# A fused attention and expert kernel: ScalarE's part of the weight conversions, moved within the step

## The chip, the cores and the metric

The kernel runs on one core of a Trainium2 chip. The metric is device time in microseconds (us); of the kernel before there are three runs and one profiled execution. The engines of the core are TensorE (PE), VectorE (DVE), ScalarE (ACT) and GpSimd (POOL); SyncE (SP) issues the transfers. Each engine takes its instructions in the order in which the program issued them.

## What is computed

Attention with two mixings of the heads, followed by an expert layer. In the reference, cut to what matters:

```python
scores = scale * np.matmul(q, k.transpose(0, 1, 3, 2))      # (8, 12, 448, 448)
scores = np.einsum('bhij,hg->bgij', scores, w_pre)
attn = np.exp(scores - np.max(scores, axis=-1, keepdims=True))
attn = attn / (np.sum(attn, axis=-1, keepdims=True) + 1e-09)
attn = np.einsum('bhij,hg->bgij', attn, w_post)
x = np.matmul(attn, v)                                      # to (3584, 768)
y = ((x @ w1) * (x @ w2) @ w3) @ w_out                      # 768 -> 1024 -> 1024 -> 768
```

The four expert weights are 64-bit floats, which the kernel reads as pairs of 32-bit integers and converts on the chip.

## The kernel before, in words

**The steps.** A batch has 448 query rows; a step handles 10 of them for all 12 heads, so a tile has 120 rows, a batch 45 steps and the kernel 360. `run` (L901 on) issues step after step, and within a step the calls stand in a fixed order; that order and the engines' queues set everything. Step n contains, with the names that the profile uses:

- VectorE's `largest(n)`: the minimum `mn` over the mixed scores `psm` (L246; the mixed scores stand there with the sign reversed, so it is the maximum that the softmax subtracts).
- ScalarE's `exp(n)`: `e` and its row sums `sm` (L253). In steps below WHOLE = 20 it is issued right behind `largest`; from step 20 on it is the last call of the step.
- `scale(n-1)`: VectorE's `sa`, `ri` (L262, L263) from the row sums, and `w` (L266), the post-mixing weights times 1/sum.
- `split_r(n+2)`: the scores of a later step in two parts, `rh` (VectorE, L226) and `rl` (GpSimd, L227).
- `qk`: scores of a later batch on TensorE (`psq`, L193, L194), copied by ScalarE to `st` (L198) and stored to DRAM (`raw_d`, L202), from where `fetch` (L217) reads them in the step's layout. In the first steps `qk_first` does the same for batch 0, with ScalarE's copies `sz` (L162, L163).
- `post(n-2)`: TensorE's `pso` (L276, eight matmuls a row block), copied by ScalarE to `mt` (L282) when `do_ends` runs near the step's end.
- `mix(n+1)`: TensorE's next `psm` (L235 in the first 20 steps, L238 to L240 after).
- in some steps `av`: the value products `psa` (L307) from `mt`, in PSUM bank 5. These steps contain no piece of a conversion.
- a share of the expert products (fold products `psf`, L365; expert products `eg`, L527, their copy `ea`, L533, and so on).

**The conversions.** `converting` (L124) is a generator that two passes of a step drive. A job is one block of a weight: `words` loads it (`cs`, L96, SyncE, three buffers) two pieces ahead; `square` (L102, ScalarE) makes `cm` from the top words, which tells where a value would be too small; `to_f32` shifts the words together on VectorE (`ca`, L112 to L114, in PSUM bank 5) and ends with `cx` (L116), which needs `cm`; `two_parts` casts `cx` to a high part on ScalarE (L121) and subtracts it on GpSimd for the low part (L122). There are 72 jobs: 40 for folding w3 with w_out (steps up to 43), then 32 unit jobs for w1 and w2 (steps 48 to 100), whose result is stored by L430 for later batches. In a piece the load of job n+2 comes in the first half of the step, and in the second half, behind the step's `exp` (below step 20), `scale`, `split_r` and `qk`:

```python
            if made:
                jobs[n - 1][1](made)        # cast and low part of job n-1
                made = None
            if 0 <= n < len(jobs):
                s = words.pop(0)
                m = self.square(s, f"{self.n_made}")
                made = self.to_f32(s, m, f"{self.n_made}")
```

The tile of the square has one buffer, the tile of `cx` those of its pool.

Of the kernel before, what the change touches and what calls it, by code (L numbers as in the profile page):

```python
# [6 lines left out]
F32 = mybir.dt.float32  # L7
# [18 lines left out]
WHOLE = 20  # L26
FIRST = 48
CW = 384
# [17 lines left out]
class Kernel:  # L46
# [51 lines left out]

    def square(self, s, name):
        n = s.shape[1]  # L100
        m = self.cx.tile([128, CW], F32, tag="m", name=f"cm{name}", bufs=1)[:, :n]
        self.nc.scalar.activation(m, s[:, :, 1].bitcast(F32), AF.Square)  # L102
        return m

# [16 lines left out]
        self.nc.scalar.copy(hi, x)  # L121
        self.nc.gpsimd.tensor_tensor(lo, x, hi.bitcast(F32), op=ALU.subtract)  # L122

    def converting(self, jobs):  # L124

        words, made = [], None
        jobs = list(jobs)
        for n in range(-2, len(jobs) + 1):  # L130
            if n + 2 < len(jobs):
                src = jobs[n + 2][0]
                words.append(self.words(src, f"{self.n_words}"))
                self.n_words += 1
            yield
            if made:
                jobs[n - 1][1](made)
                made = None
            if 0 <= n < len(jobs):
                s = words.pop(0)  # L140
                m = self.square(s, f"{self.n_made}")
                made = self.to_f32(s, m, f"{self.n_made}")
                self.n_made += 1
            yield

# [598 lines left out]
    def run(self):  # L746
        nc, tc = self.nc, self.tc
        self.kqs, self.parts, self.rs, self.rhl, self.psm, self.mns, self.es, self.w2s = ({} for _ in range(8))
        self.mt, self.vs, self.xs, self.fw = {}, {}, {}, {}
        self.later, self.ends, self.soon = [], [], []  # L750
        self.slot, self.free, self.keep, self.x_made, self.n_groups = {}, list(range(N_UP)), [], [0] * B, 0
        self.jobs, self.ys, self.pairs = [], {}, False
        dp = self.pool("dram", 1, space=DRAM)
# [62 lines left out]
        for b in range(1, B):  # L816
            first, per, ahead = (12, 26 / 48, 2) if b == 1 else ((b - 1) * NB - 6, 45 / 48, 3)
            for u in range(H * NJ):
                h, c = divmod(u, NJ)
                n = first + int(u * per)  # L820
# [36 lines left out]
        for pair in range(ONE // 2, B // 2 - 1):  # L857
            first = P_AT if pair == ONE // 2 else 2 * NB * (pair + 1) + 13
# [5 lines left out]
        def advance(count):  # L864
            nonlocal done
            for _ in range(min(count, total - done)):
                next(background)
                done += 1

        def there(p):  # L870

            f, r = divmod(p - 3 - 2 * KF, 3)
            return 2 * KF * 3 * (1 + f) + (0, 9, 18)[r] if f >= 0 else min(max(3 * (p - 3), 0), KF * 3)
# [3 lines left out]
        def others(p):  # L877
            nc.sync.dma_start(self.kq0s[p][:, JT + S:], self.kq0[p][:, JT + S:])
# [17 lines left out]
        self.unit_list = self.units()  # L896
        self.n_one, self.w_made = len(self.unit_list), 4 * KF
        self.unit_list += self.pair_units()
        unit_pieces, phases = self.converting(self.unit_jobs()), list(self.phases())
        nq, n_pieces = 0, -2  # L900
        for n in range(N + 6):  # L901
            self.step = n
            if n == GB + 1:
                self.close("qp")
                self.xp = [self.pool("xp0", 1)]
            if n == SWITCH:
                assert done == total
                next(background, None)
                self.do_ends()
                self.do_soon()  # L910
                self.do_later()
                assert not fold_pieces
                self.close("fp")
                self.wp = self.pool("wp", 5, side="right")
                self.up = self.pool("up", 1, side="right")
                self.xp.append(self.pool("xp1", 1, side="right"))
                background, total, done = self.experts(phases), (E_1 + E_2) * ONE + P_1 * (B - ONE) // 2, 0
            if n == LATE:
                assert done >= E_1
                self.close("xp0", "cx")  # L920
                self.xq, self.cb = self.pool("xq", 2), self.pool("cb", 1)
            if n == PAIR:

                assert done >= 2 * E_1 + E_2 and unit_pieces is None and not self.jobs and not self.ys
                self.do_ends()
                self.do_soon()
                self.do_later()
                self.pairs, self.w_ahead = True, 4
                self.close("xp1", "cb", "xq", "cs")
                self.xq = self.pool("xq", 2)  # L930
                self.up2 = self.pool("up2", 1, side="right")
                self.free += range(N_UP, NS)
                setup = self.pair_setup(phases)
            if PAIR <= n < PAIR + 7:
                next(setup, None)
            if LF <= n + LF < N:
                self.fetch(n + LF)
            self.do_later()
            if n + 3 < HP:
                others(n + 3)  # L940
            elif 2 * HP - 3 <= n < 2 * HP:
                self.load_v()
            for x in loads.get(n, []):
                self.load_kq(*x)

            p, pieces = self.n_made - 1 if fold_pieces else 2 * KF + 3 * KF, None
            if avs.get(n):
                pass
            elif fold_pieces:
                f = (self.n_made - 1 - 2 * KF) // 3  # L950
                if f < 2 or done >= 2 * KF * 3 * (f - 1):
                    pieces = fold_pieces
                    if next(pieces, self) is self:
                        fold_pieces = pieces = None
            for x in splits.get(n, []):
                self.split_kq(*x, nc.gpsimd, nc.gpsimd)
            if n < N:
                self.largest(n)
            if n < WHOLE:
                self.exp(n)  # L960


            if 0 <= n - 1 < N:
                self.scale(n - 1)
            if n + 2 < N:
                self.split_r(n + 2)
            self.do_soon()
            for x in firsts.get(n, [])[:1]:
                self.later.append(self.qk_first(*x, (next(turn), next(turn))))
            for x in qks.get(n, []):  # L970
                store = self.qk(*x, nq % 2, nc.scalar.copy)
                nq += 1
                if store:
                    self.later.append(store)
            if pieces:
                next(pieces)
            elif unit_pieces and not fold_pieces and not avs.get(n):
                ahead = 1 if n < SWITCH else 2 * done // (3 * K1) + 4 + (done > 0)
                if n_pieces < ahead:
                    n_pieces += 1  # L980
                    if next(unit_pieces, self) is self:
                        unit_pieces = None
                    else:
                        next(unit_pieces)
            now = share.get(n, 0)
            if n < SWITCH:

                wanted += now
                now = max(min(there(p), KF * 3 + wanted) - done, 0)
            self.do_sums()  # L990

            advance(now // 2)
            if 0 <= n - 2 < N:
                self.post(n - 2)
            for x in firsts.get(n, [])[1:]:
                self.later.append(self.qk_first(*x, (next(turn), next(turn))))
            for x in avs.get(n, []):
                self.av(*x)
            advance(now - now // 2)
            if n + 1 < N:  # L1000
                self.mix(n + 1)
            self.do_ends()

            if WHOLE <= n < N:
                self.exp(n)

        self.do_soon()
        self.do_later()
# [61 lines left out]
```

## Time and profile before

| what | value |
|---|---|
| median of 3 runs | 1633.44 us (1632.39 to 1634.12) |
| profiled execution | 1632.78 us, span 1631.0 us |
| TensorE busy | 1577.8 us, 97% of the span |
| VectorE busy | 1028.6 us, 63% |
| ScalarE busy | 1054.1 us, 65% |
| GpSimd busy | 1070.3 us, 66% |
| DMA | 436.47 MB, mean 268 GB/s |

How to read it: the shares are means over stages with different limits. The chain that ended last, followed back from the last instruction, covers only the end of the span, so the stages before it are read from a table of windows: for each stretch of the span the busy time of each engine, the granted clock of TensorE and the share of the DMA engines. In a timeline each row is an instruction with its start, its duration and, in brackets, the idle time of the engine just before it and what ended that idle time.

### The profile page before, as it was taken

To read this page: it belongs to the slowest core of one execution; us is meant where nothing else is said; L and a number is where in the kernel's file an instruction comes from. 1 tells how busy PE (TensorE), PEld (TensorE's weight loads), DVE (VectorE), ACT (ScalarE), POOL (GpSimd) and SP (SyncE) were. 2 spreads that over 40 slices of the span, in tenths; PEclk is the share of its full clock that TensorE was granted. 3 is DMA by queue.
4 is the path that set the end of the run, shared out by engine and by line. 5 is a ranking of instruction groups with operands and counts; after the bars stand their busy time and mean duration, and the time that the engine had idled before them with its cause. 6 is when DMAs were issued, how large, how long until landed. Compare 5 with 4: busy or idle time off the path is not lost. (4 is left out here: it accounts for less than half of the span.)

```text
span 1631.0 us, 31804 instructions
## 1 busy us (share of the span) xinstructions
PE 1577.8 (97%) x10528; PEld 1414.0 (87%) x10528; DVE 1028.6 (63%) x2302; ACT 1054.1 (65%) x2497; POOL 1070.3 (66%) x904
## 2 busy tenths in 40 slices
PE   6989998999999999999999999999999999999999
PEld 2569997888898888889999899998999898999988
DVE  5858668778857777763465465755565557634573
ACT  3878767777867777777776676776775554542321
POOL 1347556667757788885577777876675666655774
PEclk7999999999999999999999999999999999999999
DMA  8989869998899999999988888889988766678875
GB/s 266 339 253 278 248 206 296 288 292 275 255 291 301 315 322 309 312 331 309 304 241 280 266 244 243 247 248 307 291 247 254 233 185 204 203 228 297 279 235 180
DMA packets 233906, 436.47 MB, mean 268 GB/s; under 512 B 21838, under 2 KB 159054, under 8 KB 233678
## 3 DMA queue, kind: packets, MB, share of 16 engines
q1 hardware_dynamic: 233742, 434.44, 84.4%
q8 instruction: 84, 1.38, 0.4%
q14 instruction: 80, 0.66, 0.1%
HBM read 300.27 MB, written 134.09 MB: 266 GB/s over the span
## 5 line engine op out<-in xcount | busy, mean ns | idle before, releaser
L227 POOL TENSOR_TENSOR rl<-r,rh 120x448 fp32r<-120x448 f32 (+1 forms) x340 | 423.7, 1246 | 303.7 <-DVE rh L226 84.5
L246 DVE TENSOR_REDUCE mn<-psm 120x1 f32<-120x448 f32 x360 | 223.8, 622 | 382.7 <-PE psm L240 373.7
L276 PEld LDWEIGHTS pso<-w,e 120*112 120x112 f32 (+1 forms) x2880 | 345.3, 176 | 44.3 <-ACT mt L282 28.3
L276 PE MATMUL pso<-w,e 120*112 120x120 f32 (+1 forms) x2880 | 357.7, 267 | 17.1 <-ACT mt L282 15.2
L707 PE MATMUL e<-eh,wu 128*128 128x448 f32 x1008 | 304.6, 371 | 0.4 <-DVE c L661 0.4
L268 ACT ACTIVATE w<-wpo,ri 120x120 f32<-120x120 f32 (+1 forms) x253 | 99.9, 395 | 224.7 <-DVE ri L263 223.3
L253 ACT ACTIVATE e<-psm,mn 120x448 f32<-120x448 f32 x360 | 230.4, 640 | 18.8 <-DVE mn L246 18.2
L282 ACT COPY mt<-pso 112x480 f32<-112x480 f32 x360 | 204.8, 569 | 45.1 <-PE pso L276 43.8
L707 PEld LDWEIGHTS e<-eh,wu 128*128 128x128 f32 x1008 | 187.2, 188 | 15.3 <-DVE c L661 0.8
L226 DVE CAST rh<-r 120x448 fp32r<-120x448 f32 (+1 forms) x340 | 191.4, 563 | 2.1 <-DMA r<-raw_d 1.6
L198 ACT COPY st<-psq 112x448 f32<-112x448 f32 x336 | 172.1, 523 | 29.1 <-PE psq L194 12.2
L707 PE MATMUL e<-el,wu 128*128 128x448 f32 x504 | 187.3, 372 | 2.7 <-POOL el L646 2.7
L183 POOL TENSOR_TENSOR ql<-kq,qh 64x448 fp32r<-64x448 f32 x84 | 100.4, 1195 | 99.8 <-ACT qh L180 80.2
L307 PE MATMUL psa<-mt,v 112*64 112x150 f32 (+1 forms) x2304 | 156.9, 292 | 3.5 <-DVE cx L116 2.4
L307 PEld LDWEIGHTS psa<-mt,v 112*64 112x64 f32 x2304 | 143.6, 137 | 9.8 <-DVE cx L116 3.0
L661 DVE TENSOR_TENSOR c<-c,e 128x448 f32<-128x448 f32 x168 | 101.3, 616 | 70.7 <-PE e L707 66.2
L193 PE MATMUL psq<-kk,qh 128*112 128x448 f32 x336 | 125.0, 372 | 6.5 <-ACT st L198 6.4
L238 PE MATMUL psm<-rh,wph 120*120 120x448 f32 (+1 forms) x340 | 129.7, 382 | 0.0
L527 PE MATMUL eg<-xh,wu 128*128 128x448 f32 x384 | 127.4, 381 | 0.0
L240 PE MATMUL psm<-rl,wph 120*120 120x448 f32 (+1 forms) x340 | 124.0, 365 | 1.0 <-POOL rl L227 1.0
L239 PE MATMUL psm<-rh,wpl 120*120 120x448 f32 (+1 forms) x340 | 124.2, 365 | 0.0
L194 PE MATMUL psq<-kk,ql 128*112 128x448 f32 x336 | 122.8, 365 | 0.0
(116 smaller groups left out, 3015.4 us busy)
## 6 DMA issues: line engine op xcount, KB each, us to landing
r<-raw_d SPq DMA_DIRECT2D x352, 210.0 KB, 5.2
raw_d<-st SPq DMA_DIRECT2D x168, 392.0 KB, 4.6
wu<-w_d SPq DMA_DIRECT2D x104, 384.0 KB, 5.5
wu<-s_d SPq DMA_DIRECT2D x96, 384.0 KB, 4.6
v<-v SPq DMA_DIRECT2D x144, 224.0 KB, 4.4
wu<-w_d SPq DMA_DIRECT2D x51, 512.0 KB, 6.1
kq<-kq SPq DMA_DIRECT2D x42, 448.0 KB, 6.3
wu<-s_d SPq DMA_DIRECT2D x36, 512.0 KB, 4.5
```

What stands on the lines that cost most here:

```text
L193: nc.tensor.matmul(p, qh[:, cols], kk, start=True, stop=False)
L198: copy(st[:, c % 2], p)
L226: nc.vector.tensor_copy(rh[:K], r[:K])
L227: nc.gpsimd.tensor_tensor(rl[:K], r[:K], rh[:K].bitcast(F32), op=ALU.subtract)
L238: nc.tensor.matmul(p[:K, :S], self.wph[:K, :K], rh[:K], start=True, stop=False)
L246: nc.vector.tensor_reduce(mn[:K], p[:K, :S], axis=AX.X, op=ALU.min)
L253: nc.scalar.activation(e[:K], p[:K, :S], AF.Exp, bias=mn[:K], scale=-1.0, accum_out=sm[:K])
L276: nc.tensor.matmul(p[:, j, :, :w], e[:K, j * JT:(j + 1) * JT], w2[:K, :, :w], start=True, stop=True)
L282: self.ends.append((4, lambda: copy(dst, p[:, :, :, :w])))
L307: nc.tensor.matmul(self.psa[rows, g % 3, :W], v[:, j, rows], mt[:, j, 2 * g + s, :W], start=(j == 0), stop=(j == NJ - 1))
L527: nc.tensor.matmul(p, u[:, k % (K1 // 2), x], xs[y][:, k], start=(k == 0 and t == 0), stop=(k == K1 - 1 and t == 2))
L707: nc.tensor.matmul(p, w[:, k, x], ops[m, k][y], start=(k == 0 and t == 0), stop=(k == nk - 1 and t == 2))
```

## The change

The square of a conversion, its cast and its low part change their place in the step; VectorE's part and TensorE's work do not. `converting` gets a flag `late`. For the fold jobs (flag off) the cast and low part of job n−1 and the square of job n are issued in the first half of the piece while the step is below WHOLE, ahead of the splits and of `exp`; from step 20 on they stand where they were. For the unit jobs (flag on) they become a third part of the piece, which `run` drives at the very end of a step, behind `exp`; the square is then that of job n+1, a piece ahead. The tile of the square gets the pool's number of buffers, two, instead of one.

```diff
--- before.py
+++ after.py
@@ -98,7 +98,7 @@
 
     def square(self, s, name):
         n = s.shape[1]
-        m = self.cx.tile([128, CW], F32, tag="m", name=f"cm{name}", bufs=1)[:, :n]
+        m = self.cx.tile([128, CW], F32, tag="m", name=f"cm{name}")[:, :n]
         self.nc.scalar.activation(m, s[:, :, 1].bitcast(F32), AF.Square)
         return m
 
@@ -121,27 +121,42 @@
         self.nc.scalar.copy(hi, x)
         self.nc.gpsimd.tensor_tensor(lo, x, hi.bitcast(F32), op=ALU.subtract)
 
-    def converting(self, jobs):
-        words, made = [], None
+    def converting(self, jobs, late=False):
+        words, made, m = [], [], None
         jobs = list(jobs)
+        def parts(n):
+            if 0 <= n < len(jobs):
+                jobs[n][1](made.pop(0))
+        def square(n):
+            return self.square(words[0], f"{n}") if 0 <= n < len(jobs) else None
         for n in range(-2, len(jobs) + 1):
             if n + 2 < len(jobs):
-                src = jobs[n + 2][0]
-                words.append(self.words(src, f"{self.n_words}"))
+                words.append(self.words(jobs[n + 2][0], f"{self.n_words}"))
                 self.n_words += 1
+            first = self.step < WHOLE
+            if first and not late:
+                parts(n - 1)
+                m = square(n)
             yield
-            if made:
-                jobs[n - 1][1](made)
-                made = None
+            if not first and not late:
+                parts(n - 1)
+                m = square(n)
             if 0 <= n < len(jobs):
-                s = words.pop(0)
-                m = self.square(s, f"{self.n_made}")
-                made = self.to_f32(s, m, f"{self.n_made}")
+                made.append(self.to_f32(words.pop(0), m, f"{self.n_made}"))
                 self.n_made += 1
             yield
+            if late:
+                parts(n - 1)
+                m = square(n + 1)
+                yield
 
 
 
@@ -748,6 +763,7 @@
         self.kqs, self.parts, self.rs, self.rhl, self.psm, self.mns, self.es, self.w2s = ({} for _ in range(8))
         self.mt, self.vs, self.xs, self.fw = {}, {}, {}, {}
         self.later, self.ends, self.soon = [], [], []
+        self.step = 0
         self.slot, self.free, self.keep, self.x_made, self.n_groups = {}, list(range(N_UP)), [], [0] * B, 0
         self.jobs, self.ys, self.pairs = [], {}, False
         dp = self.pool("dram", 1, space=DRAM)
@@ -896,10 +912,10 @@
         self.unit_list = self.units()
         self.n_one, self.w_made = len(self.unit_list), 4 * KF
         self.unit_list += self.pair_units()
-        unit_pieces, phases = self.converting(self.unit_jobs()), list(self.phases())
+        unit_pieces, phases = self.converting(self.unit_jobs(), True), list(self.phases())
         nq, n_pieces = 0, -2
         for n in range(N + 6):
-            self.step = n
+            self.step, third = n, False
             if n == GB + 1:
                 self.close("qp")
                 self.xp = [self.pool("xp0", 1)]
@@ -982,6 +998,7 @@
                         unit_pieces = None
                     else:
                         next(unit_pieces)
+                        third = True
             now = share.get(n, 0)
             if n < SWITCH:
 
@@ -1003,6 +1020,8 @@
 
             if WHOLE <= n < N:
                 self.exp(n)
+            if third:
+                next(unit_pieces)
 
         self.do_soon()
         self.do_later()
```

The lines of the changed kernel behind the conversions are shifted: the copies `sz` are L177 and L178 there, `st` L213, `exp` L268, `mt` L297; the casts of a split are L195 to L197.

ScalarE around step 8, in the opening. `fo` is the high part of a fold job, `psz` and `sz` are the scores of batch 0. Before:

```order
L121 CAST fo_146<-cx9_540 128x384
L102 ACTIVATE cm10_578<-cs10_458 128x384
L282 COPY mt0_0_361<-pso5_587 112x48x10
L253 ACTIVATE e8_604,sm8_605<-psm8_594,mn8_602 120x448
L162 COPY sz4_2_617<-psz4_2_0_613 112x448
L163 COPY sz4_2_617<-psz4_2_1_614 112x448
L121 CAST fo_146<-cx10_584 128x384
L102 ACTIVATE cm11_622<-cs11_512 128x384
L282 COPY mt0_0_361<-pso6_631 112x48x10
```

And now:

```order
L297 COPY mt0_0_361<-pso5_587 112x48x10
L121 CAST fo_146<-cx10_584 128x384
L102 ACTIVATE cm11_604<-cs11_512 128x384
L268 ACTIVATE e8_608,sm8_609<-psm8_594,mn8_606 120x448
L177 COPY sz4_2_621<-psz4_2_0_617 112x448
L178 COPY sz4_2_621<-psz4_2_1_618 112x448
L297 COPY mt0_0_361<-pso6_631 112x48x10
```

The cast of job 10 and the square of job 11 moved from behind the score copies to ahead of the exponential of step 8.

ScalarE at the end of step 16, before:

```order
L198 COPY st1_2_0_1036<-psq1_2_0_1033 112x448
L198 COPY st1_2_0_1036<-psq1_2_1_1038 112x448
L121 CAST fo_146<-cx18_996 128x384
L102 ACTIVATE cm19_1044<-cs19_908 128x384
L282 COPY mt0_0_361<-pso14_1052 112x48x10
L253 ACTIVATE e17_1065,sm17_1066<-psm17_1057,mn17_1063 120x448
```

And now:

```order
L297 COPY mt0_0_361<-pso13_998 112x48x10
L121 CAST fo_146<-cx18_996 128x384
L102 ACTIVATE cm19_1017<-cs19_908 128x384
L195 CAST qh1_3_1019<-kq1_1_694 64x448
L196 CAST kk1_3_1020<-kq1_1_694 64x448
L197 CAST qh1_3_1019<-kq1_1_694 64x448
L268 ACTIVATE e16_1028,sm16_1029<-psm16_1003,mn16_1026 120x448
L213 COPY st1_2_0_1040<-psq1_2_0_1037 112x448
L213 COPY st1_2_0_1040<-psq1_2_1_1042 112x448
L297 COPY mt0_0_361<-pso14_1052 112x48x10
L268 ACTIVATE e17_1065,sm17_1066<-psm17_1057,mn17_1063 120x448
```

The score copies of step 16 are now followed at once by the copy of pso 14; cast and square stand ahead of the casts of a split.

ScalarE in steps 55 to 57, in the units' stage (`wu` is a unit's high part; in the changed kernel the number of a unit job's `cm` counts from 0, so cm6 belongs to cs46). Before:

```order
L282 COPY mt1_0_3018<-pso53_3481 112x48x10
L253 ACTIVATE e55_3494,sm55_3495<-psm55_3436,mn55_3448 120x448
L198 COPY st2_4_2_3463<-psq2_4_3_3512 112x448
L533 COPY ea0_0_3532<-eg0_0_0_3359 128x448
L282 COPY mt1_0_3018<-pso54_3520 112x48x10
L253 ACTIVATE e56_3535,sm56_3536<-psm56_3489,mn56_3500 120x448
L198 COPY st2_5_0_3556<-psq2_5_0_3553 112x448
L121 CAST wu5_3560<-cx45_3476 128x3x128
L102 ACTIVATE cm46_3563<-cs46_3413 128x384
L282 COPY mt1_0_3018<-pso55_3574 112x48x10
```

And now:

```order
L297 COPY mt1_0_3020<-pso53_3478 112x48x10
L268 ACTIVATE e55_3491,sm55_3492<-psm55_3433,mn55_3450 120x448
L121 CAST wu4_3494<-cx44_3421 128x3x128
L102 ACTIVATE cm6_3497<-cs46_3415 128x384
L213 COPY st2_4_2_3465<-psq2_4_3_3514 112x448
L548 COPY ea0_0_3534<-eg0_0_0_3356 128x448
L297 COPY mt1_0_3020<-pso54_3522 112x48x10
L268 ACTIVATE e56_3537,sm56_3538<-psm56_3486,mn56_3502 120x448
L213 COPY st2_5_0_3558<-psq2_5_0_3555 112x448
L297 COPY mt1_0_3020<-pso55_3571 112x48x10
```

The square of job 46 moved from step 57 to the end of step 55, ahead of three other instructions and the exponential of step 56. On TensorE and VectorE the order is the same in both kernels; on GpSimd the low parts of fold jobs come ahead of the splits' subtractions in steps 10 to 19, and on SyncE one load and one fetch change places in the fold jobs' stretch.

## Rows read from the trace of the kernel before

**Rows 1.** Windows by stage: us, engines' busy time (x instructions), PEclk, DMA share, GB/s.

```profile
36.09:65.89 29.80, 29.26 (x145) 16.04 (x141) 25.62 (x65) 24.16 (x59) 8.03 (x9) 0.99 0.99 332
65.89:100.43 34.54, 26.83 (x115) 14.39 (x115) 25.39 (x59) 30.48 (x70) 16.06 (x16) 0.95 0.94 312
100.43:243.11 142.68, 142.22 (x1018) 134.57 (x1019) 98.14 (x253) 101.66 (x236) 82.32 (x76) 1.00 0.80 241
243.11:440.15 197.04, 184.94 (x1322) 165.01 (x1321) 163.29 (x414) 149.46 (x348) 132.30 (x119) 1.00 0.91 286
440.15:1631.00 1190.85, 1174.29 (x7890) 1076.36 (x7888) 699.85 (x1482) 735.71 (x1760) 826.84 (x678) 1.00 0.84 265
```

The engines in the row are PE, PEld, DVE, ACT and POOL, in this order.

**Rows 2.** Waits over the whole span: us in total, times, longest.

```profile
DVE cx L116 <- ACT cm L102: 14.9, 18, 3.6
```

**Rows 3.** Timeline of step 8, ScalarE and VectorE: start, us, instruction [idle before].

```profile
58.57 0.62 DVE L246 TENSOR_REDUCE mn<-psm 120x1 f32<-120x448 f32 x1
...
59.23 0.64 ACT L253 ACTIVATE e<-psm,mn 120x448 f32<-120x448 f32 x1 [0.76 <-DVE mn L246]
...
61.10 0.57 ACT L102 ACTIVATE cm<-cs 128x384 f32<-128x384 f32 x1
...
61.77 0.55 DVE L116 SCALAR_TENSOR_TENSOR cx<-cm,ca 128x384 f32<-128x384 f32 x1 [0.33 <-ACT cm L102]
...
62.24 0.62 DVE L246 TENSOR_REDUCE mn<-psm 120x1 f32<-120x448 f32 x1
```

**Rows 4.** SyncE's store at 79.32 and its time to landing.

```profile
79.32 0.32 SPq L202 DMA_DIRECT2D raw_d<-st  x1
...
raw_d<-st SPq DMA_DIRECT2D x1, 392.0 KB, 5.1
```

**Rows 5.** Timeline of ScalarE, 84 to 100 us.

```profile
84.54 0.97 ACT L198 COPY st<-psq 112x448 f32<-112x448 f32 x2 [1.60 <-DMA raw_d<-st]
...
92.87 0.64 ACT L253 ACTIVATE e<-psm,mn 120x448 f32<-120x448 f32 x1 [0.76 <-DVE mn L246]
...
98.89 0.53 ACT L121 CAST fo<-cx 128x384 fp32r<-128x384 f32 x1
...
99.76 0.57 ACT L282 COPY mt<-pso 112x480 f32<-112x480 f32 x1
```

**Rows 6.** Timeline of TensorE from 100.38 us.

```profile
100.38 1.07 PE L276 MATMUL pso<-w,e 120*112 120x120 f32 x8 [0.65 <-ACT mt L282]
101.38 3.28 PE L307 MATMUL psa<-mt,v 112*64 112x150 f32 x48
```

**Rows 7.** Waits from 243.11 to 440.15 us.

```profile
DVE mn L246 <- PE psm L240: 24.9, 11, 3.7
...
PE pso L276 <- ACT mt L282: 6.4, 10, 1.6
```

**Rows 8.** Timeline of TensorE at the value products of step 62.

```profile
294.28 3.28 PE L307 MATMUL psa<-mt,v 112*64 112x150 f32 x48 [0.63 <-DVE cx L116]
```

**Rows 9.** Job 46: its load and landing, and steps 56's exponential and sum.

```profile
268.39 0.93 SPq L96 DMA_DIRECT2D cs<-w  x1
...
cs<-w SPq DMA_DIRECT2D x1, 384.0 KB, 7.9
...
275.57 0.64 ACT L253 ACTIVATE e<-psm,mn 120x448 f32<-120x448 f32 x1 [0.93 <-DVE mn L246]
...
276.86 0.15 DVE L262 TENSOR_SCALAR sa<-sm 120x1 f32<-120x1 f32 x1
```

**Rows 10.** DMA issues from 254 to 290 us: the unit loads, median to landing.

```profile
cs<-w SPq DMA_DIRECT2D x8, 384.0 KB, 6.3
```

**Rows 11.** GpSimd and VectorE at 255 us, and VectorE's scaling at 272 us.

```profile
255.36 1.14 POOL L183 TENSOR_TENSOR ql<-kq,qh 64x448 fp32r<-64x448 f32 x1 [3.20 <-ACT qh L180]
...
255.40 1.18 DVE L266 TENSOR_SCALAR w<-wpo,ri 120x120 f32<-120x120 f32 x1
...
272.07 0.28 DVE L266 TENSOR_SCALAR w<-wpo,ri 120x120 f32<-120x120 f32 x1
```

## The prediction

> **What bounds the kernel now.** I read the stages first, then the waits inside each stage, then the timeline at the places where ScalarE changes. The table by stage [rows 1] splits the span at four moments. From 100.43 us to 243.11 TensorE is busy 142.22 of 142.68 us, and from 440.15 to the end 1174.29 of 1190.85: no faster ScalarE can shorten these two stretches, which only slide with the moment at which they begin. What is left is the opening (to 100.43) and the stage from 243.11 to 440.15, in which the 32 unit jobs are converted.
>
> In the opening the reader should look at one step of the ring [rows 3]: VectorE's minimum at 58.57, ScalarE's exponential at 59.23, the two score copies and the cast, the square at 61.10, VectorE's last conversion instruction at 61.77 and the next minimum at 62.24. A step takes 3.67 us, and VectorE waits 0.33 us in it for the square. Over the whole run that wait comes to 14.9 us in 18 places [rows 2], nearly all of them here. But the DMA engines are at a share of 0.99 from 36 to 66 us [rows 1], so the ring is not alone in setting the pace.
>
> In the units' stage VectorE is busy 163.29 of 197.04 us and TensorE 184.94 [rows 1]. Neither is full over the stage; they take turns. Between two value products VectorE goes without a gap; at the products it waits for TensorE, 24.9 us in 11 places [rows 7]. One such product, at 294.28, itself waited 0.63 us for the last conversion instruction on VectorE, which holds the bank they share [rows 8].
>
> **The change part by part.**
>
> *A second buffer for the square.* It adds no instruction. It lets a square be written while the one before is still read; without it the square ahead would wait for VectorE. I cost it at nothing.
>
> *The opening, steps 0 to 19.* Per step a cast and a square move ahead of the exponential; none is added. The square leaves the ring, which could save up to the 0.33 us a step seen in [rows 3], and at most the 14.9 us of [rows 2]. Most of this I do not book, because of what comes at the end of the opening. ScalarE's score copies at 84.54 waited 1.60 us for a store of the scores to free their buffer [rows 5]. That store was issued at 79.32 and took 5.1 us to land [rows 4], in a stretch whose DMA share, 0.94 over 34.54 us, leaves little room [rows 1]. A ring that runs faster reaches this buffer earlier and waits longer. So I take the landing at about 84.4 us as fixed and count only what follows it.
>
> From 84.54 ScalarE runs nearly without a pause to the copy of the mixed weights at 99.76, which releases TensorE's post products at 100.38; at 101.38 the first value products start, and TensorE is full from there [rows 5, 6]. On this path two things go away. In step 16 the cast at 98.89 and the square behind it stood before that copy at 99.76, and now stand behind it: 99.76 − 98.89 = 0.87 us. And ScalarE's idle 0.76 us ahead of the exponential at 92.87 is filled by a cast and a square that now stand there: 0.76 us. Together −1.6 us. The bounds are −0.9 (if the idle time only moves to the next step) and −3.2 (if the wait of 1.60 goes as well, since the store then is also issued earlier). I take the value between, since nothing in the rows says that the store is issued earlier behind full DMA engines.
>
> *Steps 20 to 47.* The order on every engine is what it was. TensorE is full, the shift passes through: 0.
>
> *The units' stage, gain.* Here cast and square move behind the copy of the mixed weights and behind the exponential. TensorE waits 6.4 us in 10 places for that copy [rows 7], and these waits should shrink by most of a cast and a square each. I cost this at 0. The work that hides it is VectorE's: the stalls lie in steps between two value products, where VectorE has no gap and TensorE, once released, would only run into the next minimum's bank. If that cover were gone, 6.4 us would be won; that is a rival below.
>
> *The units' stage, cost.* The square of a job now stands one unit piece earlier, its load does not. So ScalarE may meet words that have not landed, and behind the waiting square stand a score copy, a copy of an expert product, the copy of the mixed weights and the next exponential. Job 46 is the case: its load is issued at 268.39 and takes 7.9 us [rows 9], so it lands at 276.3. The square now follows the exponential of step 55, which ends about 273.2, and so waits some 2.5 us. Starting at 276.3, with 0.44 us from one ScalarE start to the next (half of the 0.87 above), the square and three more stand before the exponential of step 56: 276.3 + 4 × 0.44 = 278.1 in place of 275.57, and it ends 0.64 later, at 278.7. VectorE wants its sum at 276.86 [rows 9], in the midst of the stretch that has no gap up to the value product of [rows 8]: 278.7 − 276.86 = 1.9 us lost, and the product is late by as much. The bounds are 0 (the load lands 2 us sooner) and 6.4 more (rival 3). The other unit loads of that stretch land in 6.3 us at the median [rows 10]; by the same subtraction their words are there, four of them (jobs 43, 44, 45, 48) with less than 1 us to spare.
>
> *GpSimd's low parts.* They follow the casts. In the opening they come before the splits' subtractions in steps 10 to 19, in the units' stage their order is unchanged. Here one row speaks against the change: VectorE's scaling of the mixing weights took 1.18 us at 255.40, when GpSimd's subtraction ran from 255.36 to 256.50, and 0.28 us at 272.07 [rows 11]. If the low parts, now later in the step, fell on that instruction, each hit would cost 0.9 us. I take 0: in the units' stage the low part stands behind the low part of the scores on GpSimd's queue, and that has not moved; the other end is rival 4. The Trainium skill (GPSIMD Engine Reference, § 1. Specifications) says that the two engines share their interface to SBUF, with contention for some kinds of VectorE instructions; by that rule alone a moved low part may cost as rival 4 has it, and the trace agrees for the pair at 255.40.
>
> *SyncE.* The loads and stores keep their order in the units' stage. A store of a converted unit waits for its low part; as that does not move, neither does the score fetch behind it.
>
> **The sum.** −1.6 + 1.9 = +0.3 us. The profiled execution took 1632.78 us (span 1631.0), so it would take 1633.1. It stands 0.66 below the median of the three runs, 1633.44; on the median the sum gives **1633.7 us**. About 0.2%, 3.3 us, is what a measurement of this kernel can tell from no change: the forecast is no change.
>
> **The rivals.**
>
> 1. *The waits in the units' stage were real.* For it: TensorE, not VectorE, is the busier engine of that stage, 184.94 of 197.04 us, and VectorE waits 24.9 us for it [rows 1, 7]. If every stall of TensorE delays a minimum, −1.6 − 6.4 = −8.0: 1625.4. Against it: the value product that waits for VectorE [rows 8]. If only half counts, about 1629.
>
> 2. *The words are there in time.* Loads land in 6.3 us at the median [rows 10], and 268.39 + 6.3 = 274.7 is 1.6 us earlier than job 46's did. Then the cost falls to about 0.3 or nothing: 1631.8, and 1630.2 if the store's wait goes too. Against it: the DMA engines are at 0.91 in that stage [rows 1], and the load is issued in the same place.
>
> 3. *Slower: words late in more squares.* The mechanism is that of job 46, at four more jobs in the same stage. If their loads too took 7.9 us, 1.6 more than the median, each would be late by 1.0 to 1.6 us, and VectorE's chain with it: +4 to +6.4 us, so 1637.7 to 1640.1. It decides once a landing takes over about 7.3 us. For it: the loads compete with score fetches and stores at a DMA share of 0.91, and ScalarE delays that shift the score stores shift the loads too. Against it: it needs four loads to be as slow as the slowest.
>
> 4. *Slower by far: low parts on the scaling.* If in each of the 32 unit jobs the low part met VectorE's scaling as the subtraction did at 255.40, 32 × 0.9 = 29 us at most would be added: up to 1663. Against it: GpSimd's order in that stage is the same.
>
> That the change does not do what it says is out: the order of the instructions shows every cast and square in its new place, and TensorE's and VectorE's orders as they were.
>
> **How the numbers follow.** The forecast gets 0.42, rival 2 0.18, rival 1 0.20, rival 3 0.18, rival 4 0.02. The first two lie within 0.2%, but for the tip of rival 2 (0.05) and the ends of the forecast's own bounds. Rival 1 is faster, rivals 3 and 4 slower, by over 0.2%. So faster 0.25, same 0.53, slower 0.22. The range from 1627.0 to 1639.0 takes in the larger half of rival 1 and of rival 3, leaves out rival 4, and with it some 0.17.
>
> **What would show it.** Right: VectorE's wait for the square in the opening nearly gone, yet the score copies near 84.5 waiting longer than 1.60; the post products of 100.38 some 1.6 us earlier; TensorE's waits for the mixed weights' copy after 243 well below 6.4 with VectorE's wait for TensorE grown in their place; near 275 a square that waits about 2.5 us for its words, and VectorE waiting about 1.9 for the exponential behind it. Wrong: post products of step 17 earlier by 3 us or more, or not at all; a stage of units that is shorter by several microseconds (rival 1); several squares waiting for DMA (rival 3), or none (rival 2).

## The result, and the profile after

The changed kernel is slower: a median of 1636.22 us (1632.30 to 1639.79, 13 runs) against 1632.93 us (1631.05 to 1635.98, 13 runs), a ratio of 1.0022 with a 95% interval of 1.0013 to 1.0031, or 3.6 us (2.1 to 5.1). Its profiled execution took 1635.94 us, with a span of 1633.9; that of before had 1631.0. The two profiles so differ by 2.9 us, close to the 3.6 us of the ratio, and can be compared.

The table by stage, cut at the same minima (those of steps 2, 10, 17, 48 and 102) as the rows of before [rows 1]. The columns are the stretch, its length, the busy time of PE, PEld, DVE, ACT and POOL with instructions, PEclk, DMA share, GB/s:

```profile
35.12:67.17 32.05, 31.88 (x152) 17.82 (x152) 28.81 (x65) 24.51 (x58) 7.64 (x8) 0.97 0.98 328
67.17:102.92 35.75, 28.19 (x111) 15.73 (x111) 24.89 (x59) 30.21 (x69) 16.00 (x15) 0.86 0.91 285
102.92:245.20 142.28, 141.84 (x1017) 134.19 (x1016) 98.87 (x254) 101.93 (x237) 82.08 (x75) 1.00 0.81 245
245.20:442.44 197.24, 184.88 (x1322) 165.17 (x1321) 162.73 (x414) 148.80 (x347) 132.07 (x119) 1.00 0.91 284
442.44:1633.90 1191.46, 1174.69 (x7891) 1076.38 (x7889) 700.99 (x1482) 734.66 (x1760) 826.89 (x678) 1.00 0.84 265
```

The loss stands in the first two rows: steps 2 to 9 take 32.05 us in place of 29.80, and steps 10 to 16 take 35.75 in place of 34.54. Less the 0.97 us by which step 2 began earlier, that is 2.49 us at step 17. The stages after it differ by −0.40, +0.20 and +0.61. In the first row VectorE's busy time has grown from 25.62 to 28.81 us, with the same 65 instructions. The timeline of step 8 shows in which instruction (VectorE, ScalarE's cast and exponential, GpSimd):

```profile
59.03 0.62 DVE L261 TENSOR_REDUCE mn<-psm 120x1 f32<-120x448 f32 x1
59.15 0.51 ACT L121 CAST fo<-cx 128x384 fp32r<-128x384 f32 x1 [1.16 <-DVE cx L116]
59.73 1.01 POOL L122 TENSOR_TENSOR fo<-cx,fo 128x384 fp32r<-128x384 f32 x1 [3.05 <-ACT fo L121]
59.94 0.88 DVE L281 TENSOR_SCALAR w<-wpo,ri 120x120 f32<-120x120 f32 x1
60.02 0.61 ACT L268 ACTIVATE e<-psm,mn 120x448 f32<-120x448 f32 x1
...
62.62 0.56 DVE L116 SCALAR_TENSOR_TENSOR cx<-cm,ca 128x384 f32<-128x384 f32 x1
63.09 0.62 DVE L261 TENSOR_REDUCE mn<-psm 120x1 f32<-120x448 f32 x1
```

The square no longer holds VectorE: its 0.33 us of [rows 3] are gone, and the wait comes to 2.9 us over the whole span, where before it was 14.9 [rows 2]:

```profile
DVE cx L116 <- ACT cm L102: 2.9, 3, 1.5
```

But the cast now stands right behind the conversion that it reads, so GpSimd's low part starts at 59.73, and VectorE's scaling `w`, which starts at 59.94 in the midst of it, takes 0.88 us. It ends at 60.82, 0.08 us behind the low part (60.74). The step takes 63.09 − 59.03 = 4.06 us, where it took 3.67. In steps 4 to 10 six of the scalings take 0.87 or 0.88 us and one 0.40, together 3.7 us more than at 0.28 each. VectorE has next to no gap left in step 8, and ScalarE waits for it, 1.16 us before the cast: the engine that the change was to relieve of a wait became the bound. Over steps 2 to 9 the net loss is 2.25 us.

Step 10 loses as much again, 2.21 us (7.18 us in place of 4.97), and here it is TensorE that is late:

```profile
70.98 1.56 PE L172 MATMUL psz<-kqz 64*112 64x448 f32 x2 [2.78 <-ACT sz L177]
72.47 1.85 PE L250 MATMUL psm<-r,wsc 120*120 120x448 f32 x2
...
74.35 0.62 DVE L261 TENSOR_REDUCE mn<-psm 120x1 f32<-120x448 f32 x1 [2.59 <-PE psm L250]
```

```profile
72.00:74.00 2.00, 2.00 (x3) 0.47 (x2) 0.00 (x0) 1.43 (x4) 0.00 (x0) 0.50 1.04 364
```

TensorE waits 2.78 us for a score copy, where before it was 1.03. The mix that makes the next `psm` takes 1.85 us in place of 1.01, at a granted clock of 0.50, that is 1.2 GHz (the columns of the second fence are those of the table above), and VectorE's minimum of step 11 waits 2.59 us for it. The windows from 72 to 78 us are all at 0.50; before, only the one from 72 to 74 us was. At step 11 the changed kernel is 3.49 us late. The other two kernels below in which the scaling is hit in steps 6 to 9 with this order of VectorE, the opening part alone and the changed kernel with own buffers, show the same wait (2.75 and 2.76 us); those of the third and fourth experiment, in which it is not hit, wait 1.21 and 1.28. No run separates what the wait costs from what the clock costs.

A second stretch of this kind lies at 94 us:

```profile
89.90 1.01 PE L291 MATMUL pso<-w,e 120*112 120x120 f32 x8
...
94.22 0.46 PE L208 MATMUL psq<-kk,qh 128*112 128x448 f32 x1 [2.56 <-ACT st L213]
...
95.14 1.89 PE L291 MATMUL pso<-w,e 120*112 120x120 f32 x8
```

TensorE waits 2.56 us for a score copy, and the post products after it take 1.89 us where the same eight took 1.01 just before. The windows of 2 us around it (same columns as above):

```profile
92.00:94.00 2.00, 0.00 (x0) 0.00 (x0) 1.34 (x5) 1.98 (x6) 1.47 (x2) 1.00 0.95 310
94.00:96.00 2.00, 1.78 (x8) 1.42 (x9) 1.22 (x3) 2.00 (x6) 0.39 (x1) 0.80 1.05 329
96.00:98.00 2.00, 2.00 (x9) 1.46 (x7) 0.56 (x1) 2.00 (x6) 0.61 (x1) 0.50 0.91 309
```

After the stretch in which TensorE did nothing its granted clock is 0.50 until about 98.5 us. The granted clock of the second stage is 0.86 as against 0.95 in [rows 1]. But this second stretch is not what makes the kernel late. On ScalarE the same instructions stand between the two score copies in both kernels, and take as long (88.34 to 93.61 us, before 84.54 to 89.80); only the copy `mt` has moved to their front, so that two waits of TensorE, 0.62 us at 86.87 and 1.71 us at 90.41 before, have become one. And ScalarE is busy 13.37 of the 13.50 us from 88.34 to 101.84, so it does not wait for the slower TensorE.

### The profile page after: what moved, and what is told of

It reads as the page before. It is cut to its first block, busy times and chain, and to the rows that moved or that the text cites. A ratio compares the mean times of both kernels' runs of the same rounds, so it can differ in the third digit from the quotient of the medians.

```text
span 1633.9 us, 31795 instructions
## 1 busy us (share of the span) xinstructions
PE 1579.9 (97%) x10528; PEld 1415.7 (87%) x10528; DVE 1032.6 (63%) x2302; ACT 1053.2 (64%) x2497; POOL 1069.9 (65%) x904
## 5 line engine op out<-in xcount | busy, mean ns | idle before, releaser
L297 ACT COPY mt<-pso 112x480 f32<-112x480 f32 x360 | 205.0, 569 | 51.4 <-PE pso L291 50.2
L268 ACT ACTIVATE e<-psm,mn 120x448 f32<-120x448 f32 x360 | 229.9, 639 | 8.7 <-DVE sa L277 6.0
L213 ACT COPY st<-psq 112x448 f32<-112x448 f32 x336 | 171.8, 523 | 26.1 <-DMA raw_d<-st 12.5
```

What stands on the lines that cost most here:

```text
L213: copy(st[:, c % 2], p)
L268: nc.scalar.activation(e[:K], p[:K, :S], AF.Exp, bias=mn[:K], scale=-1.0, accum_out=sm[:K])
L297: self.ends.append((4, lambda: copy(dst, p[:, :, :, :w])))
```

## The experiments

All ratios below are to the kernel before, run on the same chip beside the kernel in question, with a 95% interval; 0.0010 is 1.6 us. The theories: **A**, the loss arises in the opening, by GpSimd's low part on VectorE's scaling. **B**, it arises in the units' stage, by late words. **C**, it is the order on VectorE or ScalarE by itself. **D**, the end of the opening is held by the store that frees a buffer of `st`.

**The opening part alone.** Edit:

```diff
-        unit_pieces, phases = self.converting(self.unit_jobs(), True), list(self.phases())
+        unit_pieces, phases = self.converting(self.unit_jobs()), list(self.phases())
...
-                        third = True
```

> Only the opening part of the change (fold jobs: cast, low part and square ahead of the exponential in the first 20 steps); the unit jobs stand as in the kernel before. Theory A (the loss arises in the opening: GpSimd's low part now meets VectorE's scaling w, 0.88 us in place of 0.28, and late score copies idle TensorE until its clock falls): the whole loss stays, +2.5 to +4 us against before, steps 6 to 9 take 4.05 us each. Theory B (the loss arises in the units' stage, by words that land late): no loss, within 1 us of before.

Measured: 1635.87 us, ratio 1.0013 (1.0004 to 1.0022), some 2.1 us, a little less than A said. The scaling takes 0.87 or 0.88 us in the same steps, and steps 6 to 9 take 3.60 to 4.06 us each. Its trace, of an execution of 1634.26 us, shows that what follows the ring varies: the eight steps from 2 to 9 cost 2.05 us more than before there too, but no score copy waits for a store behind them, and at step 20 that execution is only 0.30 us late. Another 1.5 us of its time stand at step 77, where the value products run at a granted clock of 0.67. Two more kernels show that in their traces, the scaling ahead with own buffers and the square ahead with own buffers (0.65 and 0.64, 1.7 us each); the kernel before does not (1.00). That the whole loss is the opening's is thus shown here by the medians; the trace shows it only up to step 10.

**The units' part alone.** Edit:

```diff
-            first = self.step < WHOLE
+            first = False
```

> Only the units' part of the change (cast, low part and the square ahead at the end of a step); the opening stands as in the kernel before. Theory A: within 1 us of before, since the minima keep their distance to before's from step 20 to step 100 to some 0.3 us. Theory B: +2 to +4 us, with squares that wait for their words.

Measured: 1633.29 us, ratio 1.0000 (0.9990 to 1.0010). Four squares of it wait for their words in the units' stage, 3.7 us in all, and the time is that of before. Theory B falls: by these two medians the loss is the opening's. The two parts sum to less than the whole (2.1 us of 3.6), but within the intervals.

**Only the square ahead, cast and low part where they were.** Edit, on the opening part alone:

```diff
             if first and not late:
-                parts(n - 1)
                 m = square(n)
             yield
+            if not late:
+                parts(n - 1)
             if not first and not late:
-                parts(n - 1)
                 m = square(n)
```

> Opening: only the square goes ahead of the exponential, the cast and the low part stay behind the score copies; unit jobs as before. Theory A: the scaling w is back at 0.28 us in steps 6 to 9 and VectorE no longer waits 0.33 us for the square, so these steps take some 3.45 us; the total lies between -2 and +1 us against before. If the mere presence of more ScalarE work ahead of the exponential is what costs (theory C), steps 6 to 9 stay above 3.66 us and the total at +1 us or more.

Measured: 1631.41 us, ratio 0.9989 (0.9981 to 0.9998): faster than before. GpSimd and VectorE in steps 7 and 8 of this kernel:

```profile
57.10 1.00 POOL L122 TENSOR_TENSOR fo<-cx,fo 128x384 fp32r<-128x384 f32 x1 [2.45 <-ACT fo L121]
57.37 0.55 DVE L116 SCALAR_TENSOR_TENSOR cx<-cm,ca 128x384 f32<-128x384 f32 x1
57.84 0.62 DVE L261 TENSOR_REDUCE mn<-psm 120x1 f32<-120x448 f32 x1
58.75 0.28 DVE L281 TENSOR_SCALAR w<-wpo,ri 120x120 f32<-120x120 f32 x1
...
61.31 0.62 DVE L261 TENSOR_REDUCE mn<-psm 120x1 f32<-120x448 f32 x1
```

The low part runs from 57.10 to 58.10, the scaling at 58.75 takes 0.28 us, and the step 61.31 − 57.84 = 3.47 us. So the square ahead alone gives the 0.2 us a step that VectorE's other work allows, and moving the cast with it is what turns this into a loss.

**The scaling ahead of the minimum.** The changed kernel with its cast and low part left in their new place, and VectorE's order altered instead:

```diff
+            if n < WHOLE and n > 0:
+                self.scale(n - 1)
             if n < N:
                 self.largest(n)
...
-            if 0 <= n - 1 < N:
+            if WHOLE <= n and n - 1 < N:
                 self.scale(n - 1)
```

> The changed kernel, but in the first 20 steps VectorE's sa, ri and w stand ahead of the minimum in place of behind it, so that w is over before the low part starts. Theory A: w back at 0.28 us in steps 6 to 9, these steps at some 3.45 to 3.5 us in place of 4.05; the total 1 to 3 us below the changed kernel's. Theory C: steps 6 to 9 stay at about 4.05 us and the total at +2.5 us or more against before.

Measured: 1632.19 us, ratio 0.9998 (0.9988 to 1.0007), some 3.9 us below the changed kernel by the ratios, more than was expected. VectorE and GpSimd:

```profile
57.57 0.28 DVE L281 TENSOR_SCALAR w<-wpo,ri 120x120 f32<-120x120 f32 x1
57.77 0.62 DVE L261 TENSOR_REDUCE mn<-psm 120x1 f32<-120x448 f32 x1
57.89 1.00 POOL L122 TENSOR_TENSOR fo<-cx,fo 128x384 fp32r<-128x384 f32 x1 [2.46 <-ACT fo L121]
...
61.23 0.62 DVE L261 TENSOR_REDUCE mn<-psm 120x1 f32<-120x448 f32 x1
```

With the scaling over before the low part starts, the step takes 3.46 us, and the minimum, which lies beside the low part now, still takes 0.62. At step 14 this kernel is 6.1 us ahead of before, yet only 1.2 at step 18. In between its score copies wait and TensorE with them:

```profile
83.36 0.96 ACT L213 COPY st<-psq 112x448 f32<-112x448 f32 x2 [2.47 <-DMA raw_d<-st]
...
98.80 4.63 PE L322 MATMUL psa<-mt,v 112*64 112x150 f32 x48
```

That is the wait of [rows 5], longer because the engine came to it earlier, and further on the 48 value products, 3.28 us in [rows 6], take 4.63, at a granted clock of 0.54 and 0.60 in the windows from 98 to 102 us.

**The kernel before with the scaling ahead.** The same two edits of `run` on the kernel before, as a control.

> The kernel before with sa, ri, w ahead of the minimum in the first 20 steps and nothing else. Theory A: the low part comes behind the score copies here and hits w only in a few steps (1.08, 0.84, 0.71, 0.92 us in steps 9, 11, 13, 15), while steps 6 to 9 stay at 3.66 us or grow by the later minimum (up to 0.6 us): within 2 us of before, no gain like that of 3.6 us in the changed kernel. Theory C (order on VectorE by itself): a gain of 2 us or more.

Measured: 1638.50 us, ratio 1.0031 (1.0021 to 1.0041), worse than the 2 us allowed for. Steps 6 to 9 take 4.23 us: there the minimum still starts ScalarE's chain, and it comes later by sa, ri and w. So the order on VectorE by itself wins nothing; in the changed kernel it wins because it takes `w` out of the low part's way. Theory C falls.

**Both cures at once.** The square ahead alone, with the scaling ahead as well.

> Both cures at once: in the first 20 steps only the square goes ahead of the exponential (cast and low part behind the score copies, as before) and VectorE's sa, ri, w stand ahead of the minimum; unit jobs as before. Theory A (the loss is GpSimd's low part on w): no w over 0.4 us in steps 2 to 16, steps 6 to 9 at 3.45 us, total -1.5 to -3 us against before, no better than the square alone (-1.8) by more than 1 us if the wait for the score store near 83 us stays. Theory C (order on VectorE matters by itself): worse than the square alone.

Measured: 1633.01 us, ratio 0.9998 (0.9989 to 1.0007): a miss. The scaling takes 0.53 or 0.54 us in steps 5 to 10 and steps 6 to 9 some 3.72 us each. Its rows show why:

```profile
58.35 1.00 POOL L122 TENSOR_TENSOR fo<-cx,fo 128x384 fp32r<-128x384 f32 x1 [2.71 <-ACT fo L121]
58.89 0.54 DVE L281 TENSOR_SCALAR w<-wpo,ri 120x120 f32<-120x120 f32 x1
```

With the cast in its old place the low part runs at the end of the step, and the scaling moved to the front of the next meets it there: each cure alone keeps the two apart, the two together bring them together again. `w` ends at 59.43, 0.08 us behind the low part.

**Own buffers for the score copies, on the changed kernel with the scaling ahead, and on the kernel before.** From step 12 on the copies `sz` use the other pool's two buffers. Edit (on the kernel before the same, with the step read where it is known):

```diff
-            st = (self.qp if p % 2 else self.kp).tile([JT, 2, S], F32, tag="st", name=f"sz{p}_{c}", bufs=2)
+            st = (self.qp if p % 2 or self.step >= 12 else self.kp).tile([JT, 2, S], F32, tag="st", name=f"sz{p}_{c}", bufs=2)
```

> The changed kernel with sa, ri, w ahead of the minimum, and from step 12 on the copies sz of batch 0 use the other pool's two buffers, so that the copies st have their two to themselves. Theory D (what a faster opening wins is held up by the store that frees the buffer of st near 83 us, and by TensorE's clock after it): the wait of 2.5 us for the store near 83 us is gone, TensorE keeps 2.4 GHz from 84 to 88 us, and the total falls 1 to 3 us below that of the run with sa, ri, w ahead alone (-0.3 us). If something else holds the opening (the DMA engines at their limit): the wait only moves to another copy or fetch, and the total stays within 1 us of it.

> The kernel before, and from step 12 on the copies sz use the other pool's two buffers, so that st has two to itself. Theory D: the wait of 1.60 us for the store at 84.5 us is gone and the total falls by 0.5 to 2 us. If the DMA engines hold the opening: within 0.5 us of before, with the wait elsewhere.

Measured: 1631.37 us, ratio 0.9984 (0.9976 to 0.9993), and 1631.24 us, ratio 0.9987 (0.9978 to 0.9995). In both no score copy waits for a store any more before 110 us, and both gain about 2 us over the kernel that they were made from. Theory D holds: that wait was on the path. The clock was expected to stay up in the first of them from 84 to 88 us; it is at 1.00 from 82 to 86 us, but falls after: its mean from 86 to 90 us is 0.88 and from 90 to 94 us 0.69.

**The changed kernel with own buffers and nothing else.** The last edit on the changed kernel.

> The changed kernel with nothing but the own buffers for st from step 12 on. Theory A with D: w is still at 0.88 us and steps 6 to 9 at 4.05 us; only the wait of 2.03 us for the store at 88.3 us goes, so the total stays 0 to +3 us against before, above the run that also has sa, ri, w ahead (-2.6 us) by 2 us or more. If the store's wait was the whole loss: -2 us or less, like that run.

Measured: 1635.18 us, ratio 1.0014 (1.0006 to 1.0023). Steps 7 to 9 take 4.05 or 4.06 us, the scaling 0.87 or 0.88. So the wait for the store was not the loss; the gain of some 2 us on the other kernels is here 1.3 by the ratios, within the noise of those two.

Three pairs of these kernels differ in whether the scaling meets the low part: the changed kernel and the one with the scaling ahead (1.0022 and 0.9998), the same two with own buffers (1.0014 and 0.9984), and the opening part with and without the cast moved (1.0013 and 0.9989). They are 3.9, 4.9 and 3.9 us apart.

**The square ahead and own buffers.** The edits of the square ahead and of the own buffers together, unit jobs as before.

> The two gains together: only the square goes ahead of the exponential in the first 20 steps (-1.8 us alone), and from step 12 on the copies sz use the other pool's buffers (-2.1 us alone on the kernel before); unit jobs as before. If the two are separate costs: -3 to -4 us against before, steps 6 to 9 at 3.45 us and no wait of st for a store near 83 us. If the second only catches what the first brings to the same place (DMA engines or TensorE's clock hold the end of the opening): about -2 us.

Measured: 1628.21 us (1627.14 to 1631.68), ratio 0.9971 (0.9960 to 0.9981), 4.7 us below before and the best of all: the gains of 1.8 and 2.1 us are separate and add up. (Its profiled execution took 1631.68 us and contains the 1.7 us at step 77; steps 6 to 9 take 3.45 to 3.47 us, and no score copy waits for a store before 110 us.)

## Why the prediction was right or wrong

The range held the result. The likeliest case, no change, did not come: the kernel is 2.1 to 5.1 us slower, while the sum said +0.3. That the range held it is luck: what made the kernel slower stood in the prediction as rival 4, outside the range and in another stage.

*The opening, −1.6 us: wrong, in sign.* Post products and value products of step 17 come 2.1 us later, not 1.6 us earlier (102.52 and 103.48 us, before 100.38 and 101.38). The step that failed is the one on GpSimd's low parts, "I take 0": it looked at the order on GpSimd's queue in the units' stage alone, and for the opening it named only the splits' subtractions. It had the row that prices the meeting, 1.18 us in place of 0.28 [rows 11], and gave it 0.02 as rival 4, in the wrong stage. In the opening GpSimd is idle most of the time (busy 8.03 of 29.80 us [rows 1]), so its low part starts as soon as the cast is done; a cast moved from the end of the step to right behind the conversion puts it under the scaling, 0.6 us in each of six steps. Experiments three and four show this from either side. The Trainium skill (SBUF — State Buffer, § SBUF: two separate sides) says that for VectorE instructions in a two-port mode, or with two inputs in SBUF, the pair of ports shared with GpSimd is an exclusive lock: whichever engine starts first keeps it for its whole instruction, and the other one waits. The trace agrees for the scaling: every one that is lengthened ends 0.07 to 0.09 us after GpSimd's instruction, at 60.82 against 60.74 in step 8. So the price is the rest of GpSimd's instruction.

*The landing held near 84.4 us: wrong as a fixed time.* The score copies do wait longer than 1.60 us, 2.03, but they start at 88.34 us in place of 84.54, 3.80 us later, since the ring, slower in steps 2 to 10, issued the store at 83.55 in place of 79.32:

```profile
83.55 0.32 SPq L217 DMA_DIRECT2D raw_d<-st  x1
...
88.34 0.97 ACT L213 COPY st<-psq 112x448 f32<-112x448 f32 x2 [2.03 <-DMA raw_d<-st]
...
101.84 0.59 ACT L297 COPY mt<-pso 112x480 f32<-112x480 f32 x1
102.52 1.03 PE L291 MATMUL pso<-w,e 120*112 120x120 f32 x8
```

The kernels with a faster ring show the case that was argued: 2.47 us at 83.36 in the fourth experiment. That the wait swallows what the ring wins was right; that it was on the path, and could be taken away, is new from the experiments with own buffers.

*The path behind it, 0.87 + 0.76 us: right in size.* From the score copies to the value products it took 16.84 us before (84.54 to 101.38) and takes 15.14 now (88.34 to 103.48): 1.70 us less, where 1.63 was said. Of this, 0.85 us is won where the first copy `mt` no longer waits for cast and square (1.71 us behind the score copies, now 0.86), and 0.92 in the round from one `mt` to the next in which the idle 0.76 us is filled. In step 16 itself, where the prediction placed the 0.87, nothing is won: cast and square left the end of that round and stand at its front, and ScalarE, which has no gap there, needs 4.62 us for it in place of 4.57. So the time comes out as 3.80 − 1.70 = 2.10 us late at the value products: the term of −1.6 was there, but it started from a landing that had moved.

*The units' stage, gain 0: right.* TensorE's waits for the weights' copy shrank from 6.4 us in 10 places [rows 7] to 1.8 in 2, and the stage did not get shorter (197.24 us against 197.04); the waits moved instead. ScalarE's copy now waits for TensorE, 11.3 us where it was 5.3, and VectorE's wait for TensorE went from 24.9 us to 25.6:

```profile
DVE mn L261 <- PE psm L255: 25.6, 10, 3.7
ACT mt L297 <- PE pso L291: 11.3, 18, 1.5
ACT cm L102 <- DMA cs<-w: 4.6, 4, 1.9
PE pso L291 <- ACT mt L297: 1.8, 2, 1.5
```

The run with this part alone stands at 1.0000.

*The units' stage, cost +1.9 us: right in its mechanism, off in its size.* Job 46 is where it was said to be:

```profile
277.34 0.55 ACT L102 ACTIVATE cm<-cs 128x384 f32<-128x384 f32 x1 [1.92 <-DMA cs<-w]
...
279.07 0.66 ACT L268 ACTIVATE e<-psm,mn 120x448 f32<-120x448 f32 x1
279.86 0.15 DVE L277 TENSOR_SCALAR sa<-sm 120x1 f32<-120x1 f32 x1 [0.88 <-ACT e L268]
```

The square waits 1.92 us for its words (about 2.5 was said) and VectorE 0.88 for the exponential (1.9 was said). Its load took 7.0 us, not 7.9, which is most of the difference. Nor did the 0.88 last: the lag behind before goes from 2.03 us at the minimum of step 57 to 2.71 at step 58 and 2.19 at step 59. One step later the kernel before loses what this one does not, a scaling of 0.84 us at 281.25 that takes 0.30 here. Net, the stage cost 0.20.

*The rivals.* Rival 1 was not seen: the waits of TensorE in the units' stage were not on the path. Rival 3's waits were there, in part: four squares wait for their words, 4.6 us in all, but the stage does not lose by it. Rival 2's price came true for that stage, not its cause, since the words were not in time.

## What to carry to other kernels

When an instruction on one engine moves, follow the one that it releases on another, into every stage: here a cast on ScalarE carried a subtraction on GpSimd under VectorE's scaling, and 0.6 us of blocked VectorE a step outweighed the 0.2 us won. Take the piece of a change that removes the wait (the square) apart from the piece that rides along (the cast); the first alone was faster, the two together slower. Where a gain disappears at a buffer that a store still holds, give that work a buffer of its own: the two changes together were worth 4.7 us where the first alone gave 1.8.

## What was not expected of the hardware

VectorE's instructions on the same stretch are hit very unequally: under GpSimd's subtraction the scaling (120x120, from SBUF) goes from 0.28 to as much as 1.20 us, while the minimum over a PSUM tile keeps its 0.62 us and the conversion's last instruction its 0.56. And TensorE's granted clock fell to 0.50 behind a wait of 2.56 us at 94.22, until about 98.5 us; TensorE had been busy 1.66 us of the window from 90 to 92. The same work with two waits of 0.62 and 1.71 us kept it at 1.00 in the kernel before. The last wait alone does not tell it: behind the same 0.82 us the value products of step 77 ran at 1.00 in the kernel before and at 0.67 with the opening part alone. What decides there is not shown.
